# Cosine attention into a token and channel MLP on one core: PSUM split anew, and a pair's scores in one group

## The chip, the core and the metric

The kernel runs on one core of a Trainium2 chip. A core has a matrix engine (TensorE, "PE" in the profile), two engines that read its results from PSUM (VectorE, "DVE", and ScalarE, "ACT"), a fourth engine that works in SBUF alone (GpSimd, "POOL"), and SyncE ("SP"), whose queue issues most of the DMAs. Each engine works through its own list of instructions in order; semaphores hold an instruction back until what it needs is there. PSUM has eight banks of 128 partitions by 512 fp32 numbers. The metric is device time in microseconds (us).

## The reference, cut to what matters

```python
def _attn_ref(q, k, v, tau):              # 8 batches, 12 heads, 448 tokens, 64 columns
    q_n = q / (np.linalg.norm(q, axis=-1, keepdims=True) + 1e-06)
    k_n = k / (np.linalg.norm(k, axis=-1, keepdims=True) + 1e-06)
    scores = np.matmul(q_n, k_n.transpose(0, 1, 3, 2)) / tau
    ...
    attn = np.exp(scores)
    attn = attn / (np.sum(attn, axis=-1, keepdims=True) + 1e-09)
    return np.matmul(attn, v)

def _moe_ref(x, w_tok1, w_tok2, w_ch1, w_ch2):   # x: 8 x 448 x 768, all heads side by side
    xt = x.transpose(0, 2, 1)
    h = np.maximum(xt @ w_tok1, 0.0) @ w_tok2    # token MLP, 448 -> 256 -> 448
    u = x + h.transpose(0, 2, 1)
    h2 = np.maximum(u @ w_ch1, 0.0) @ w_ch2      # channel MLP, 768 -> 1536 -> 768
    return u + h2
```

## The kernel before

The attention part works on 48 pairs of heads, six to a batch. The 448 tokens are three blocks of 128 and a rest of 64; the two heads' rests stand together as one block of 128 partitions. For one pair p the stages are:

- **Norms.** Squares of q and k (L176; on ScalarE or GpSimd), their sums on VectorE (`sums`, L189), four small ScalarE activations that turn a sum into one over the norm (`rnorms`, L197 to L200), and the scaling to fp16 on GpSimd (`scaled`, L207).
- **Transposes** of the scaled q and k: on TensorE through a PSUM tile `pst` and a VectorE copy (`next_qk`) for pairs below 15, by DMA afterwards (`dma_tpose`).
- **Scores** (`score`, L297): for each block c of three, two matmuls, one for each head, into the two banks of a tile `psS`. A head has 64 columns, so each of these matmuls uses 64 of the 128 rows of the array, and the two of a block stand side by side in it. One exp on ScalarE empties both banks (L298). The rests go through a full-height matmul into `psX` (L304) and an exp of their own (L305).
- **Values** (`pv`, L318 and L320): 28 matmuls, in two halves of 14, each into a tile `psO` of one bank; a column of ones beside v gives the sums of the exps. VectorE takes the reciprocal (L323) and multiplies (L324), which gives x of the pair.
- **Token MLP**: `m_tok1` (tile `psR`, L338, a VectorE max) and `m_tok2` (tile `psU`, L357, then a VectorE copy or add into `ut`).

Once all six pairs of a batch have their `ut`, the channel MLP of the batch is put into a queue of units: 12 of `m_ch1` (six matmuls of 448 columns into `psG`, L385, a Relu on ScalarE, L387) and 6 to 9 of `m_ch2` (twelve matmuls of up to 384 columns into `psF`, L400, an add on VectorE, L403). `feed` takes units out of that queue and puts them between the steps of later pairs, until a budget of matmul time is used up.

The order on every engine is the order in which the program is written (the schedule is a manual one). Loop i = 0 to 49 takes one pair's scores at a time: the scores of pair i, the values of pair i-1, the first token matmul of pair i-2, the second of the same pair or of pair i-3. Three stretches are written differently: i below 6, where no channel MLP is to be had yet; i = 6 (`FIRST`); and from there on. Before the change, blocks 0 and 1 of the scores stand at the head of a pair, and block 2 later, after the values and some channel work; from i = 12 (`JOIN`) on, block 2 of an even pair stands beside block 0 of the next.

PSUM is shared out as follows. Pool `ps` has four tiles of one bank for everything but scores: `pst`, `psX`, `psO`, `psR`, `psU`, `psG`, `psF`, in turn. Pool `ps2` has two tiles of two banks for `psS`. A tile is handed out again in order: the first matmul of the fifth tile of `ps` waits until the first one's reader is done.

Of the kernel before, what the change touches and what calls it, by code (L numbers as in the profile page):

```python
# [7 lines left out]
FP32 = mybir.dt.float32  # L8
FP16 = mybir.dt.float16
# [13 lines left out]
def kernel(  # L23
# [12 lines left out]
    nc = tc.nc  # L36
# [30 lines left out]
    att = ctx.enter_context(tc.tile_pool(name="att", bufs=3))  # L67
    mix = ctx.enter_context(tc.tile_pool(name="mix", bufs=2))
    outp = ctx.enter_context(tc.tile_pool(name="outp", bufs=2))
    ps = ctx.enter_context(tc.tile_pool(name="ps", bufs=4, space=bass.MemoryType.PSUM))  # L70
    ps2 = ctx.enter_context(tc.tile_pool(name="ps2", bufs=2, space=bass.MemoryType.PSUM))

    id16 = cst.tile([P, P], FP16, name="id16")
    tiny = cst.tile([P, 1], FP32, name="tiny")
# [225 lines left out]

    def score_x(p):
        qk, pt = qks[p], pts[p % 2]
        psX = ps.tile([P, 512], FP32, name=f"psX_{p}", tag="b")
        nc.tensor.matmul(psX[:, 0:S], qk[:, P * NC:P * (NC + 1)], qk[:, 512:512 + S], start=True, stop=True)  # L304
        nc.scalar.activation(out=pt[:, PX:PX + S], in_=psX[:, 0:S], func=AF.Exp, scale=inv_tau)  # L305

    def pv(p, a):
        n, j = p // HP, p % HP
        vt, vx, pt = vts[n % NV], vxs[n % NV], pts[p % 2]
        if a == 0:  # L310
            xs[p] = att.tile([P, NC + 1, P], FP16, name=f"x_{p}", tag="x")
        psO = ps.tile([P, 2, 2 * E1], FP32, name=f"psO_{p}_{a}", tag="b")
        for mm in range(2):
            lo = P * (2 * a + mm)
            for g in range(2):
                for c in range(NC):
                    at = (2 * c + g) * S + lo
                    nc.tensor.matmul(psO[:, mm, E1 * g:E1 * (g + 1)], pt[:, at:at + P], vt[:, 2 * j + g, c, 0:E1],  # L318
                                     start=(g == 0 and c == 0), stop=False)
            nc.tensor.matmul(psO[:, mm, :], pt[:, PX + lo:PX + lo + P], vx[:, j, 0:2 * E1], start=False, stop=True)  # L320
        rec = att.tile([P, 2, 2], FP32, name=f"rec_{p}_{a}", tag="rec")
        o = psO[:].rearrange("p m (g e) -> p m g e", g=2)
        nc.vector.reciprocal(out=rec[:], in_=o[:, :, :, E])  # L323
        nc.vector.tensor_tensor(out=xs[p][:, 2 * a:2 * a + 2, :].rearrange("p m (g e) -> p m g e", g=2),  # L324
                                in0=o[:, :, :, 0:E], in1=_bcast_free(rec[:], E), op=ALU.mult)


# [4 lines left out]
                                    in_=xs[p][:].rearrange("p c d -> p (c d)"))  # L332

    def m_tok1(p):
        psR = ps.tile([P, TT, P], FP32, name=f"psR_{p}", tag="b")
        for tt in range(TT):
            for m in range(NC + 1):
                nc.tensor.matmul(psR[:, tt, :], w1t[:, m, tt * P:(tt + 1) * P], xs[p][:, m, :],  # L338
                                 start=(m == 0), stop=(m == NC))
        rs[p] = att.tile([P, TT, P], FP16, name=f"r_{p}", tag="r")  # L340
        nc.vector.tensor_scalar_max(out=rs[p][:], in0=psR[:], scalar1=0.0)

    def m_tok2(p):
        b, dt = p // NPAIR, p % NPAIR
        odd = b % 2
        if b // 2 not in pairt:
            pairt[b // 2] = (mix.tile([P, DT, 2 * S], FP16, name=f"ut16_{b // 2}", tag="ut16"),
                             mix.tile([P, CT, 2 * S], FP16, name=f"gt16_{b // 2}", tag="gt16", bufs=1))  # L350
        ut = pairt[b // 2][0][:, dt, S * odd:S * (odd + 1)]
        psU = ps.tile([P, S], FP32, name=f"psU_{p}", tag="b")
        by_dma = p in X_DMA
        lo = 0 if odd else XR
        cols = [XR * odd + P * c for c in range(NC)] + [0 if odd else SM]
        for tt in range(TT):
            nc.tensor.matmul(psU[:], rs[p][:, tt, :], w2t[:, tt, lo:lo + S], start=(tt == 0),  # L357
                             stop=by_dma and tt == TT - 1)
        if not by_dma:
            for c in range(NC + 1):  # L360
                w = P if c < NC else XR
                nc.tensor.matmul(psU[:, cols[c]:cols[c] + w], xs[p][:, c, :], id16[:, 0:w],
                                 start=False, stop=(c == NC))
            nc.vector.tensor_copy(out=ut, in_=psU[:])
        else:
            for u0, x0, w in ((0, SM, XR), (XR, 0, SM)) if odd else ((0, 0, S),):
                nc.vector.tensor_tensor(out=ut[:, u0:u0 + w], in0=psU[:, u0:u0 + w], in1=xTs[p][:, x0:x0 + w],  # L367
                                        op=ALU.add)
# [79 lines left out]


    FIRST = NPAIR  # L450

    JOIN = 2 * NPAIR
    early_sq = {3: 0, 4: 1, 5: 1, 6: 3, 7: 4, 8: 5, 9: 5, 10: 6, 11: 7, 12: 8, 13: 9, 14: 9, 15: 10, 16: 11, 17: 11}
    sq_slot = {p: early_sq.get(p, p - 6) for p in range(3, NP_ALL)}
    sq_at = at(sq_slot)
# [15 lines left out]
    cast_at = at({n: {1: 2, 2: 6}.get(n, 3 * n - 2) for n in range(1, NHALF)})  # L471
    tok_slot = {p: FIRST if p in (FIRST - 2, FIRST - 1) else p + 2 for p in range(NP_ALL)}
    tok_at = at(tok_slot)
    tok2_slot = {p: max(tok_slot[p] + (p in X_DMA), 3) for p in range(NP_ALL)}
    tok2_at = at(tok2_slot)

    ut_at = at({p: 8 + p // 3 if p < NPAIR else 12 + (p - NPAIR) // 2 if p < 2 * NPAIR else t + 1
# [31 lines left out]
    with tc.manual_schedule():  # L509
# [77 lines left out]
        for i in range(NP_ALL + 2):  # L587
# [17 lines left out]
            def next_qk(p):  # L605
                if p < min(DMA_FROM, NP_ALL):
                    qk_copy(p, tpose(p))
# [13 lines left out]

            if i == FIRST:
                next_sq([9])
                m_tok1(i - 2)
                pv(i - 1, 0)
                pv(i - 1, 1)
                tok2(i - 2)
                m_tok1(i - 1)
                next_qk(i)
                tok2(i - 1)  # L630
                norm_sums(8)
                feed(0.0, 1000.0)
                score(i, 0)
                rnorms(2, 21, 45)
                score(i, 1)
                norm_sums(9)
                feed(0.0, 1000.0)
            elif 0 < i < NP_ALL and not (i > JOIN and i % 2):
                score(i, 0, 2 if i < 4 else 0)
                score(i, 1)  # L640
            for p in sum_at.get(i, ()):
                norm_sums(p)
            if i != FIRST:
                norm_rn()

            if i >= FIRST:
                for p in sc_at.get(i, ()):
                    norm_scale(p, nc.gpsimd)
            if i < FIRST or i >= 2 * NPAIR:
                next_sq([p for p in sq_at.get(i, ()) if p != 9])  # L650
            if i < FIRST:
                for p in sc_at.get(i, ()):
                    norm_scale(p, nc.gpsimd)
            for n in cast_at.get(i, ()):
                cast_v(n)
            if i in (2, 5):
                weights_ch1(i // 4)
            if i in (7, 8):
                weights_ch2(i - 7)

            if i < FIRST:
                if i:
                    pv(i - 1, 0)
                if i:
                    score(i, 2)
                    score_x(i)
                if i + 1 < FIRST:
                    next_qk(i + 1)
                for p in tok_at.get(i, ()):
                    m_tok1(p)  # L670
                if i:
                    pv(i - 1, 1)
                for p in tok2_at.get(i, ()):
                    tok2(p)
            elif i == FIRST:
                score(i, 2)
                score_x(i)
                feed(0.0, 1000.0)
                rnorms(3, 0, 21)
                next_qk(i + 1)  # L680
                next_sq(sq_at[i])
                norm_sums(10)
                feed(0.0, 1000.0)
            else:
                feed(quota * 0.25)
                next_qk(i + 1)
                if i <= NP_ALL:
                    pv(i - 1, 0)
                for p in tok_at.get(i, ()):
                    m_tok1(p)  # L690
                feed(quota * 0.25, 400.0)
                ahead = i >= JOIN and i % 2 == 0
                if ahead and i <= NP_ALL:
                    pv(i - 1, 1)
                if i < NP_ALL:
                    if i > JOIN and i % 2:
                        score(i, 1)
                    score(i, 2)
                    if ahead:
                        score(i + 1, 0)  # L700
                    score_x(i)
                if i < 2 * NPAIR:
                    next_sq(sq_at[i])
                for p in tok2_at.get(i, ()):
                    tok2(p)
                feed(quota * 0.25)
                if i <= NP_ALL and not ahead:
                    pv(i - 1, 1)
                if i < 2 * NPAIR:
                    for p in sq_at[i]:  # L710
                        norm_sums(p)
                feed(quota * 0.25)
            if i == 2:
                place_w2()
        for p in ut_at.get(NP_ALL + 2, ()):
# [37 lines left out]
```

## Time and profile before

| | |
|---|---|
| Median of 12 runs | 399.3 us (398.94 to 401.0) |
| The profiled execution | 401.0 us, of which the span from first to last instruction is 399.1 us |
| TensorE busy | 386.3 us, 3658 matmuls |
| ScalarE, VectorE, GpSimd busy | 225.9, 205.0, 208.5 us |
| Mean granted TensorE clock | 0.987 |

The profile's page lists busy time by engine, the span in 40 slices of 10 us (each digit is a tenth, 9 is 90% or more), and the costliest groups of instructions as "line engine op out<-in shapes xcount | busy us, mean ns of one | idle time before them". A timeline row gives start, length and engine of a group of like instructions. Matmuls overlap: the next starts before the last is through, so the length of one (353 ns for 448 columns) is not what it costs; the distance between starts is. Where this text says "step", it is that distance.

### The profile page before, as it was taken

The page shows a single profiled execution, that of the slowest core. Times are in us where ns is not written, and L with a number is a line of the kernel's source. Part 1 is how long each engine was busy: PE and PEld are TensorE (multiplying, and loading weights), DVE is VectorE, ACT ScalarE, POOL GpSimd, SP SyncE. Part 2 cuts the span into 40 slices and gives each one's busy share as a digit, 9 for nine tenths or more (in the row PEclk, how much of TensorE's full clock was granted, in tenths as well). Part 3 has the DMA queues.
Part 4 walks back from the last instruction along what each step waited for, and adds up shares of the span by engine and source line. Part 5 has one row for each costly group of instructions (what it writes and reads, how often), then busy time and mean ns, then how long its engine had stood idle before and what let it go on. Part 6 is the DMA issues. An engine that isn't in the chain of part 4 may idle for free.

```text
span 399.1 us, 9143 instructions
## 1 busy us (share of the span) xinstructions
PE 386.3 (97%) x3658; PEld 228.3 (57%) x3658; DVE 205.0 (51%) x464; ACT 225.9 (57%) x407; POOL 208.5 (52%) x306
## 2 busy tenths in 40 slices
PE   7599999999999999999999999999999999999997
PEld 2256556566556565565565565565555565566554
DVE  5678778665453655446444645546544443243022
ACT  5888599753676447655657436665657435520410
POOL 4967495968292949576682919567682500000000
PEclk9779999999999999999999999999999999999999
DMA  8999999999797599898997599889953553013013
GB/s 219 254 232 245 239 228 208 208 240 270 159 182 159 137 252 196 182 201 185 230 204 178 96 263 208 166 192 195 212 109 72 137 105 68 15 41 110 10 39 118
DMA packets 137482, 67.51 MB, mean 169 GB/s; under 512 B 93216, under 2 KB 133984, under 8 KB 137440
## 3 DMA queue, kind: packets, MB, share of 16 engines
q1 hardware_dynamic: 133264, 61.36, 70.4%
q0 software_dynamic: 3632, 5.18, 7.5%
q8 instruction: 28, 0.46, 0.5%
q10 hardware_dynamic: 544, 0.39, 0.3%
q14 instruction: 14, 0.11, 0.1%
HBM read 43.38 MB, written 11.01 MB: 136 GB/s over the span
## 4 chain that ended last, share of the span: by engine, by line
PE 44%; POOL 24%; issue 17%; DMA 6%; ACT 5%; DVE 2%; SPq 1%; ACTq 0%; POOLq 0%; DVEq 0%
PE psF L400 16%; PE psG L385 13%; POOL kq L207 9%; POOL sq L176 8%; PE psO L318 4%; PE psS L297 3%; DMA xv<-in_v_dram 3%; POOL sqx L176 2%; ACT pt L298 2%; PE psR L338 2%; POOL kq L218 2%; DMA xq<-in_q_dram 2%; PE psU L357 2%; POOL vt L164 2%; PE psX L304 1%
## 5 line engine op out<-in xcount | busy, mean ns | idle before, releaser
L298 ACT ACTIVATE pt<-psS 128x896 f16<-128x896 f32 x141 | 122.1, 916 | 65.3 <-PE psS L297 65.2
L385 PE MATMUL psG<-ut,wc1t 128*128 128x448 f16 x576 | 120.7, 353 | 0.0
L400 PE MATMUL psF<-wc2t,gt 128*128 128x384 f16 (+2 forms) x684 | 116.3, 323 | 0.0
L387 ACT ACTIVATE gt<-psG 128x448 f16<-128x448 f32 x96 | 52.5, 547 | 74.5 <-PE psG L385 74.3
L207 POOL TENSOR_TENSOR kq<-km,rn 128x384 f16<-128x384 f32 x47 | 39.6, 842 | 99.7 <-ACT rn L200 98.4
L400 PEld LDWEIGHTS <-gt 128*128 128x128 f16 x684 | 64.8, 98 | 40.5 <-issue 1.1
L385 PEld LDWEIGHTS <-wc1t 128*128 128x128 f16 x576 | 53.2, 98 | 46.5 <-issue 4.4
L403 DVE TENSOR_TENSOR ost<-psF,ur 128x384 f32<-128x384 f32 (+2 forms) x57 | 31.3, 549 | 78.1 <-PE psF L400 78.1
L318 PEld LDWEIGHTS <-pt 128*128 128x128 f16 x1152 | 53.5, 98 | 15.6 <-issue 3.9
L318 PE MATMUL psO<-vt,pt 128*128 128x65 f16 x1152 | 58.4, 195 | 0.0
L189 DVE TENSOR_REDUCE ssq<-sq 128x12 f32<-128x768 f32 (+1 forms) x49 | 45.2, 931 | 17.9 <-POOL sq L176 12.8
L297 PE MATMUL psS<-qk 64*128 64x448 f16 x282 | 41.6, 363 | 2.6 <-ACT pt L298 2.5
L324 DVE TENSOR_TENSOR x<-psO,rec 128x256 f16<-128x256 f32 x96 | 40.7, 424 | 3.3
L320 PE MATMUL psO<-vx,pt 128*128 128x130 f16 x192 | 42.3, 220 | 0.0
L323 DVE RECIPROCAL rec<-psO 128x4 f32<-128x4 f32 x96 | 17.1, 178 | 48.0 <-PE psO L320 47.8
L207 POOL TENSOR_TENSOR kq<-qm,rn 128x384 f16<-128x384 f32 x47 | 38.9, 828 | 0.0
L176 POOL TENSOR_TENSOR sq<-km 128x384 f32<-128x384 f32 x42 | 34.4, 822 | 2.7 <-DMA km<-in_k_dram 2.5
L338 PE MATMUL psR<-x,w1t 128*128 128x128 f16 x384 | 29.4, 219 | 0.1
L367 DVE TENSOR_TENSOR ut<-psU,xT 128x448 f16<-128x448 f32 (+2 forms) x39 | 17.6, 477 | 20.1 <-PE psU L357 20.0
L357 PE MATMUL psU<-w2t,r 128*128 128x448 f16 x96 | 25.9, 353 | 0.7 <-DVE x L324 0.4
L305 ACT ACTIVATE pt<-psX 128x448 f16<-128x448 f32 x48 | 26.5, 553 | 0.0
L176 POOL TENSOR_TENSOR sq<-qm 128x384 f32<-128x384 f32 x30 | 24.7, 823 | 0.8
(75 smaller groups left out, 322.9 us busy)
## 6 DMA issues: line engine op xcount, KB each, us to landing
vm<-in_v_dram SPq DMA_DIRECT2D x16, 576.0 KB, 5.3
out_dram<-ost SPq DMA_DIRECT2D x23, 384.0 KB, 3.9
qm<-in_q_dram SPq DMA_DIRECT2D x15, 576.0 KB, 6.1
km<-in_k_dram SPq DMA_DIRECT2D x15, 576.0 KB, 5.1
wc1t<-in_moe_w_ch_dram POOLq DMA_DIRECT2D x2, 1152.0 KB, 13.7
wc2t<-in_moe_w_ch_dram POOLq DMA_DIRECT2D x2, 1152.0 KB, 15.0
out_dram<-ost SPq DMA_DIRECT2D x9, 192.0 KB, 3.2
xq<-in_q_dram SPq DMA_DIRECT2D x7, 192.0 KB, 5.3
```

The costliest lines, as they stand in the source:

```text
L176: eng.tensor_tensor(out=out, in0=src, in1=src, op=ALU.mult)
L189: nc.vector.tensor_reduce(out=ssqs[p // HP % 3][:, lo + 6 * a0:lo + 6 * a1], in_=sq[p][:, a0:a1].rearrange("p a g e -> p (a g) e"), axis=A ...
L207: eng.tensor_tensor(out=kqs[n % 2][:, j, a, 0:NC, :].rearrange("p c (g e) -> p g c e", g=2), in0=src, in1=_bcast_free(rn, E), op=ALU.mult)
L297: nc.tensor.matmul(psS[:, g, 0:S], qk[r, P * c:P * (c + 1)], qk[r, 512:512 + S], start=True, stop=True)
L298: nc.scalar.activation(out=pt[:, 2 * S * c:2 * S * (c + 1)].rearrange("p (g s) -> p g s", g=2), in_=psS[:, :, 0:S], func=AF.Exp, scale=inv ...
L318: nc.tensor.matmul(psO[:, mm, E1 * g:E1 * (g + 1)], pt[:, at:at + P], vt[:, 2 * j + g, c, 0:E1], start=(g == 0 and c == 0), stop=False)
L320: nc.tensor.matmul(psO[:, mm, :], pt[:, PX + lo:PX + lo + P], vx[:, j, 0:2 * E1], start=False, stop=True)
L324: nc.vector.tensor_tensor(out=xs[p][:, 2 * a:2 * a + 2, :].rearrange("p m (g e) -> p m g e", g=2), in0=o[:, :, :, 0:E], in1=_bcast_free(re ...
L338: nc.tensor.matmul(psR[:, tt, :], w1t[:, m, tt * P:(tt + 1) * P], xs[p][:, m, :], start=(m == 0), stop=(m == NC))
L385: nc.tensor.matmul(psG[:], wc1t[:, dt, ct * P:(ct + 1) * P], ut[:, dt, sp], start=(dt == 0), stop=(dt == DT - 1))
L387: nc.scalar.activation(out=gt[:, ct, sp], in_=psG[:], func=AF.Relu)
L400: nc.tensor.matmul(psF[:, 0:w], gt[:, ct, lo:lo + P], wc2t[:, ct, P * i0:P * i1], start=(ct == 0), stop=(ct == CT - 1))
```

## The change

The two pools are cut differently: `ps` keeps two tiles of one bank, for `psG`, `psF`, `pst` and, in the first two batches, `psU`; `ps2` has three tiles of two banks, in turn for `psS`, `psX`, `psO`, `psR` and the later `psU`. The three blocks of a pair's scores stand in one group, and `JOIN` is gone. `pv` is no longer in halves: all 28 matmuls go into one two-bank tile, with one reciprocal and one multiplication. The rest of a pair's order is written anew around that: the exp of `psX`, the norms (`norm_rn`, `norm_scale`), the squares and the casts of v change places, `psU` of the first pairs moves one pair later, and the portions of `feed` are cut differently. The matmuls themselves are the same 3658.

```diff
-    ps = ctx.enter_context(tc.tile_pool(name="ps", bufs=4, space=bass.MemoryType.PSUM))
-    ps2 = ctx.enter_context(tc.tile_pool(name="ps2", bufs=2, space=bass.MemoryType.PSUM))
+    ps = ctx.enter_context(tc.tile_pool(name="ps", bufs=2, space=bass.MemoryType.PSUM))
+    ps2 = ctx.enter_context(tc.tile_pool(name="ps2", bufs=3, space=bass.MemoryType.PSUM))
...
     def score_x(p):
-        psX = ps.tile([P, 512], FP32, name=f"psX_{p}", tag="b")
+        psX = ps2.tile([P, 2, 512], FP32, name=f"psX_{p}", tag="s")[:, 0, :]
...
-    def pv(p, a):
+    def pv(p):
...
-        psO = ps.tile([P, 2, 2 * E1], FP32, name=f"psO_{p}_{a}", tag="b")
-        for mm in range(2):
+        psO = ps2.tile([P, NC + 1, 256], FP32, name=f"psO_{p}", tag="s")
+        for m in range(NC + 1):
...
     def m_tok1(p):
-        psR = ps.tile([P, TT, P], FP32, name=f"psR_{p}", tag="b")
+        psR = ps2.tile([P, 2, 512], FP32, name=f"psR_{p}", tag="s")[:, 0, 0:TT * P].rearrange("p (t d) -> p t d", t=TT)
...
-        psU = ps.tile([P, S], FP32, name=f"psU_{p}", tag="b")
+        psU = (ps.tile([P, 512], FP32, name=f"psU_{p}", tag="b") if b < 2 else
+               ps2.tile([P, 2, 512], FP32, name=f"psU_{p}", tag="s")[:, 0, :])[:, 0:S]
...
-    tok2_slot = {p: max(tok_slot[p] + (p in X_DMA), 3) for p in range(NP_ALL)}
+    tok2_slot = {p: min(p + 3, FIRST) if p < NPAIR else tok_slot[p] + (p in X_DMA) for p in range(NP_ALL)}
...
             if i == FIRST:
                 next_sq([9])
+                rnorms(2, 21, 33)
+                norm_scale(7, nc.gpsimd)
+                pv(i - 1)
                 m_tok1(i - 2)
-                pv(i - 1, 0)
-                pv(i - 1, 1)
+                tok2(i - 3)
+                next_qk(i)
                 tok2(i - 2)
                 m_tok1(i - 1)
-                next_qk(i)
+                score(i, 0)
+                score(i, 1)
+                score(i, 2)
                 tok2(i - 1)
...
-            elif 0 < i < NP_ALL and not (i > JOIN and i % 2):
+            elif 0 < i < NP_ALL:
                 score(i, 0, 2 if i < 4 else 0)
                 score(i, 1)
+                score(i, 2)
...
             if i < FIRST:
+                for p in tok2_at.get(i, ()):
+                    tok2(p)
+                if i == 3:
+                    next_qk(i + 1)
                 if i:
-                    pv(i - 1, 0)
+                    pv(i - 1)
                 if i:
-                    score(i, 2)
                     score_x(i)
-                if i + 1 < FIRST:
+                if i in (0, 1, 2, 4):
                     next_qk(i + 1)
                 for p in tok_at.get(i, ()):
                     m_tok1(p)
-                if i:
-                    pv(i - 1, 1)
-                for p in tok2_at.get(i, ()):
-                    tok2(p)
...
             else:
-                feed(quota * 0.25)
+                if i >= 2 * NPAIR:
+                    next_sq(sq_at.get(i, ()))
+                if i < DMA_FROM:
+                    norm_next()
+                    casts()
+                fed[0] = 0.0
+                feed(quota * 0.3, 900.0 if i < DMA_FROM else 1800.0)
+                if i < NP_ALL:
+                    score_x(i)
+                if i >= DMA_FROM:
+                    norm_next()
+                    casts()
                 next_qk(i + 1)
                 if i <= NP_ALL:
-                    pv(i - 1, 0)
+                    pv(i - 1)
+                both = [p for p in tok2_at.get(i, ()) if p in tok_at.get(i, ())]
+                if not both:
+                    feed(quota * 0.3)
                 for p in tok_at.get(i, ()):
                     m_tok1(p)
-                feed(quota * 0.25, 400.0)
-                ahead = i >= JOIN and i % 2 == 0
-                if ahead and i <= NP_ALL:
-                    pv(i - 1, 1)
-                if i < NP_ALL:
-                    if i > JOIN and i % 2:
-                        score(i, 1)
-                    score(i, 2)
-                    if ahead:
-                        score(i + 1, 0)
-                    score_x(i)
                 if i < 2 * NPAIR:
                     next_sq(sq_at[i])
+                if both:
+                    feed(quota * 0.3, 900.0)
                 for p in tok2_at.get(i, ()):
                     tok2(p)
-                feed(quota * 0.25)
-                if i <= NP_ALL and not ahead:
-                    pv(i - 1, 1)
                 if i < 2 * NPAIR:
                     for p in sq_at[i]:
                         norm_sums(p)
-                feed(quota * 0.25)
+                feed(quota * 0.4, 900.0 if i >= 2 * NPAIR else 0.0)
```

`norm_next` is `norm_rn` and then the pair's `norm_scale`; `casts` holds the casts of v and the loads of the channel weights, which stood in the loop before.

## The prediction

> **What bounds the kernel now.** First the busy times and the clock on the page, then the groups of work:
>
> ```profile
> PE 386.3 (97%) x3658; PEld 228.3 (57%) x3658; DVE 205.0 (51%) x464; ACT 225.9 (57%) x407; POOL 208.5 (52%) x306
> ...
> PEclk9779999999999999999999999999999999999999
> ...
> L298 ACT ACTIVATE pt<-psS 128x896 f16<-128x896 f32 x141 | 122.1, 916 | 65.3 <-PE psS L297 65.2
> L324 DVE TENSOR_TENSOR x<-psO,rec 128x256 f16<-128x256 f32 x96 | 40.7, 424 | 3.3
> L323 DVE RECIPROCAL rec<-psO 128x4 f32<-128x4 f32 x96 | 17.1, 178 | 48.0 <-PE psO L320 47.8
> ```
>
> TensorE is busy 97% and the other engines about half, but overlapping matmuls hide what a step costs. So next the timeline of TensorE, in the steady part:
>
> ```profile
> 200.52 0.22 PE L320 MATMUL psO<-vx,pt 128*128 128x130 f16 x1
> 200.57 0.61 PE L338 MATMUL psR<-x,w1t 128*128 128x128 f16 x8
> ...
> 202.59 0.22 PE L320 MATMUL psO<-vx,pt 128*128 128x130 f16 x1
> 202.74 0.55 PE L297 MATMUL psS<-qk 64*128 64x448 f16 x4
> 203.23 0.36 PE L304 MATMUL psX<-qk 128*128 128x448 f16 x1
> 203.43 0.54 PE L357 MATMUL psU<-w2t,r 128*128 128x448 f16 x2
> 203.80 3.57 PE L385 MATMUL psG<-ut,wc1t 128*128 128x448 f16 x18
> 207.21 0.35 PE L318 MATMUL psO<-vt,pt 128*128 128x65 f16 x6
> ```
>
> Read the starts. 18 `psG` take 3.41 us, 189 ns each; `psX` to `psU` is 0.20. That is 448 columns at full rate, with no wait between tiles: TensorE is the bound and runs gapless. From 80 us to the end the starts of single matmuls show five gaps of over 0.1 us, 1.8 us in all. One thing costs extra without being a wait: going in and out of the half-height scores. `psO` to `psR` takes 0.055 us, the same `psO` to `psS` 0.150. Single starts give 285 against 189 out of `psG`, 258 against 162 out of `psF`, and 281 against 189 from the last score to whatever follows. So a run of scores costs 95 on entry and 93 on leaving, **188 ns a run**, whatever stands before it.
>
> The early pairs differ; some one-microsecond stretches, and two rows of ScalarE's timeline:
>
> ```profile
> 18.00:19.00 1.00, 0.00 (x0) 0.50 1.15 187
> ...
> 24.00:25.00 1.00, 1.00 (x14) 0.50 0.98 216
> 25.00:26.00 1.00, 1.00 (x12) 0.99 0.74 165
> ```
> ```profile
> 27.82 1.73 ACT L298 ACTIVATE pt<-psS 128x896 f16<-128x896 f32 x2 [0.38 <-PE psS L297]
> 29.43 0.52 ACT L174 ACTIVATE sq<-qm 128x384 f32<-128x384 f32 x1
> ```
>
> (Third and later columns of the first: TensorE busy, granted clock, DMA share, GB/s.) The clock is 0.50 from 14.9 to 25.0 us; TensorE had idled. Two exps in a row take 1.73 us: a step of 0.815, then 0.916 to the end; squares and norms stand in the same queue.
>
> **The change, part by part.**
>
> *Scores in one group.* Counting by the two instruction orders: 78 runs of half-height matmuls before (two a pair for pairs 1 to 11, 1.5 a pair for 12 to 47, two in pair 0), 49 after. 29 x 0.188 = **-5.45 us**, all on the bound engine. [...] The trace measured the step itself, so I take 0.188.
>
> *One tile for a pair's values.* VectorE does 48 reciprocals of 128x8 (about 185 ns) and 48 products of 128x512 in place of 96 and 96. From 256 to 512 columns I add 1.05 ns a column (L367: 623 at 448, 547 at 384, so 1.2; L403 384 against 256: 556 - 424, so 1.03): 690 ns. Saved 48 x (1204 - 875) = 15.8 us of VectorE, worth 0: it is half idle. The price is lateness: x of the pair is ready 0.9 us after the last `psO`, not 0.6. Readers of x come a pair later, so only the ring waits for it.
>
> *The ring of three.* A tile now waits for the reader three tiles back. Steady order: S0 S1 S2 X O R U, so X waits for exp S0, O for exp S1, R for exp S2, U for exp X, the next S0 for O's product, S1 for R's max, S2 for U's add. The hardest steady pair (14 of them put two `psG` ahead of X), from S0 = 0: scores end 0.76, G 1.9, G 3.03, X 3.23, O 4.23 (24 x 0.033 + 4 x 0.056), R 4.68, then U. ScalarE: exps 0.41 to 2.95, two Relus (547 each, step 0.43) to 3.8, exp X to 4.3. U finds its tile free at 4.3, needs it at 4.68: 0.4 to spare. VectorE: O seen 4.4, product done 5.3, max 5.7, add 6.4; the next S2 comes at 7.8. With `psF` ahead of X there is more room. **0**; if that cover goes, ScalarE at 916 and 547 without overlap puts exp X at 4.85: 0.17 x 14 = +2.4.
>
> *Two banks for the channel MLP.* Unit k waits for the reader of k-2, at least one unit later (1.13 us against a Relu of 0.55): 0 in steady state, 0.2 once at pair 12, where a `psF` meets `psU` in the same pool.
>
> *Pairs 1 to 5.* No channel work stands between S2 and the values. O waits for exp S0, X for S1, R for S2, and the next S1 for exp X, which now stands behind three exps and the norms and squares. Pair 4: exps to 2.95, four norm activations 1.0, a square 0.5, exp X to 4.95; pair 5's S1 wants its tile at 3.9: 1.1 late. Pair 1: O waits for exp S0 (19.1, as late as S2 waits now), but then 28 matmuls come, not 14: 0.4 late. Pair 3: 0.1. Walked so, the values of pair 5 start at 40.75 (now 40.72) with a `psU` (0.57) and a `psR` (0.45) still undone; the 5 runs saved (0.94) are spent too: **+2.0**. Bounds: 0 (waits as now) to +3.5.
>
> *Pairs 6 to 11.* Relus queue behind exps and norms with two `psG` banks. Pair 6's eight norm activations hold back a Relu and the exps of 7: X of 7 waits 0.75, its next `psG` 0.3; pairs 8 and 10 (norms 1.1 before the Relu) 0.6 and 0.4; 0.15 in pair 6: +2.2. Today's gaps there are 2.0; 0.75 (q and k of pair 12 come late from GpSimd) stay, the rest goes, since the transposes and scores that wait there move: -1.25. **+0.95**; bounds -0.5 to +2.5.
>
> *Pairs 12 to 47.* Half of today's 1.8 us of gaps should go with three score tiles, less the 0.2: **-0.7**.
>
> *Moved steps.* From pair 12 GpSimd takes squares before scaling, and from 15 the norms come after exp X, about 2 us later in a pair. Scaling of a half's first pair ends about 9 us after its norm pair began (norms done 5.4, five GpSimd rows 3.5); SyncE's transpose of it, issued at 6.8, then blocks SyncE some 2 us: behind it wait x and u transposes, loads issued three pairs ahead, and stores. q and k are needed two pairs (13 us) on. The last scaling of the three ends 3 us before its transpose. Casts of v are needed three pairs on. The four weight loads stay in their pairs. All 0; if GpSimd fell 5 us behind, the next norms would stand in ScalarE ahead of the Relus, some 0.5 us for each of 11 halves.
>
> Sum: -5.45 + 2.0 + 0.95 - 0.7 = -3.2. The profiled execution took 401.0 (span 399.1), so 397.8 for it; set against the median 399.3, which lies 1.7 lower, **396.1**.
>
> **Rivals.** (1) *ScalarE paces the ring.* For it: seven tiles in three places, four of them behind exps. Against: 0.4 us to spare. With the 2.4 above: 398.5. (2) *The clock stays low*, and the kernel is slower. [...] (3) *The switch isn't what costs 188 ns*, but the first matmul after a semaphore, and each new order pays it elsewhere. Against: `psO` to `psR` enters a new tile too, at 0.055. Then 399.3 + 2.0 + 0.95 - 0.7 = 401.5. (4) *The early pairs don't wait* (VectorE and ScalarE catch up): 396.1 - 2.5 = 393.6.
>
> **Numbers.** Forecast 0.52, rival 1 0.18, rival 2 0.20, rival 3 0.04, rival 4 0.06. A measurement tells 0.2% (0.8 us) from no change. Faster: 0.52 + 0.06 + two thirds of rival 1 = 0.70; same: the rest of rival 1 and 0.03 of rival 2 (two windows); slower 0.17 + 0.04 = 0.21. The likeliest case alone spans 394.0 to 398.2 (early bounds). The range, 393.5 to 400.5, leaves out the worse part of rivals 2 and 3, about 0.18.
>
> **What would show it.** Right: 49 runs of scores with 0.15 before and 0.28 after each; no gap of over 0.1 us between matmuls from 100 us on but a few; idle before `psO` of pairs 1 to 4 put down to the exp, and before S1 of pair 5; clock 1.0 from 25 to 28 us. Wrong: regular gaps before `psU` or S0 in the steady part, a clock of 0.50 beyond 28 us, or SyncE's waits on the scaling growing past 10 us.

## The result, and the profile after

The changed kernel takes **395.0 us** (median of 8 runs, 394.37 to 395.82) against 399.3 before (32 runs on the same chip): ratio 0.9888, 95% interval 0.9872 to 0.9903, so 1.1% or 4.3 us faster. The forecast was 396.1. The profiled execution took 394.9 us, its span 393.1, mean clock 0.991.

The page of the changed kernel, busy times, clock and groups:

```profile
PE 379.1 (96%) x3658; PEld 229.2 (58%) x3658; DVE 193.5 (49%) x368; ACT 225.9 (57%) x411; POOL 209.3 (53%) x306
...
PEclk9699999999999999999999999999999999999999
...
L298 ACT ACTIVATE pt<-psS 128x896 f16<-128x896 f32 x141 | 119.0, 921 | 66.1 <-PE psS L297 65.9
...
L322 DVE RECIPROCAL rec<-psO 128x8 f32<-128x8 f32 x48 | 9.9, 207 | 80.8 <-PE psO L318 80.7
...
L323 DVE TENSOR_TENSOR x<-psO,rec 128x512 f16<-128x512 f32 x48 | 33.2, 691 | 1.7
```

TensorE issues the same 3658 matmuls and is 7.2 us less busy. VectorE has 96 instructions fewer and 11.5 us less work: the wide product takes 691 ns (worked out: 690), the reciprocal 207 (185).

The timeline of TensorE in the steady part, one pair:

```profile
201.57 1.30 PE L385 MATMUL psG<-ut,wc1t 128*128 128x448 f16 x6
202.80 0.74 PE L297 MATMUL psS<-qk 64*128 64x448 f16 x6
203.48 2.44 PE L385 MATMUL psG<-ut,wc1t 128*128 128x448 f16 x12
205.76 0.35 PE L304 MATMUL psX<-qk 128*128 128x448 f16 x1
205.95 0.35 PE L316 MATMUL psO<-vt,pt 128*128 128x65 f16 x6
...
208.07 0.61 PE L337 MATMUL psR<-x,w1t 128*128 128x128 f16 x8
208.51 0.54 PE L357 MATMUL psU<-w2t,r 128*128 128x448 f16 x2
```

One run of six scores where there were two runs of four and two. `psG` to `psS` is 1.23 us: 5 x 0.189 inside the tile and 0.285 on entry. Entry and exit cost what they did (the step out of the last score is 0.281 again), but come once. `psX` to `psO` is 0.19, `psR` to `psU` 0.44: no wait. From 101.4 us to the end no single step is more than 0.06 us above full rate (0.189 us for 448 columns, 0.162 for 384, 0.056 for 128).

What TensorE waited for, costliest first (us in total, times, longest), without the first two lines, which belong to the start-up:

```profile
PE psU L357 <- DVE w2t L150: 1.3, 1, 1.3
PE psF L400 <- DVE ost L403: 1.3, 1, 1.3
PE psO L316 <- ACT pt L298: 0.9, 2, 0.6
...
PE psS L297 <- ACT pt L305: 0.5, 2, 0.4
```

The last two are of the waits foreseen in the early pairs. The first two were not foreseen. The first is `psU` of pair 0 at 27.9 us, which waits for VectorE's placing of the second token weight. The second is seen in the timeline of all engines at pairs 12 and 13:

```profile
87.44 2.53 SPq L376 DMA_TRANSPOSE ur<-ut  x2
...
90.06 1.90 SPq L410 DMA_DIRECT2D out_dram<-ost  x2
...
93.40 0.61 PE L337 MATMUL psR<-x,w1t 128*128 128x128 f16 x8
...
94.68 0.56 DVE L403 TENSOR_TENSOR ost<-psF,ur 128x384 f32<-128x384 f32 x1 [3.54 <-DMA out_dram<-ost]
...
95.30 2.11 PE L400 MATMUL psF<-wc2t,gt 128*128 128x384 f16 x12 [1.29 <-DVE ost L403]
```

Read it upwards. `psF` needs one of the two banks of the channel MLP; the bank's reader, VectorE's add into `ost`, waits 3.54 us because both `ost` buffers are still being stored; the store was issued at 90.06, behind two `ur` transposes in SyncE's queue. VectorE meanwhile holds back everything else. It costs 1.45 us of TensorE.

**Where the time went.** For every step from one matmul to the next I took what it lasted above full rate, with 188 ns for each run of scores counted as normal, and summed by stretch. The comparison is with a profiled execution of the unchanged kernel whose half-clock stretch is as long as after's (399.43 us, span 397.6, clock 0.991); the one shown before the prediction had three microseconds more of it.

| | before | after | difference | predicted |
|---|---|---|---|---|
| 29 score runs x 0.188 | | | -5.45 | -5.45 |
| 0 to 40 us (pairs 0 to 5) | 11.7 | 13.8 | +2.1 | +2.0 |
| 40 to 80 us (pairs 6 to 11) | 2.8 | 1.7 | -1.1 | +0.95 |
| 80 us to the end | 2.1 | 2.3 | +0.2 | -0.7 |
| sum | | | -4.25 | -3.2 |

The spans differ by 4.5; a quarter of a microsecond is not placed. So the mechanism is the one foreseen and two of the stretches are not.

### The profile page after: what moved, and what is told of

Read it like the earlier page. It is cut to its first block, busy times and chain, and to the rows that moved or that the text cites. A ratio compares the mean times of both kernels' runs of the same rounds, so it can differ in the third digit from the quotient of the medians.

```text
span 393.1 us, 9085 instructions
## 1 busy us (share of the span) xinstructions
PE 379.1 (96%) x3658; PEld 229.2 (58%) x3658; DVE 193.5 (49%) x368; ACT 225.9 (57%) x411; POOL 209.3 (53%) x306
## 4 chain that ended last, share of the span: by engine, by line
PE 86%; ACT 5%; DVE 4%; DMA 2%; SPq 1%; issue 1%; DVEq 0%
PE psF L400 28%; PE psG L385 27%; PE psO L316 9%; PE psS L297 7%; PE psR L337 5%; PE psU L357 4%; PE psO L318 3%; ACT pt L298 2%; PE psX L304 2%; DMA out_dram<-ost 1%; DMA km<-in_k_dram 1%; PE psU L362 1%; PE pst L239 1%; DVE ost L403 1%; DVE ssq L189 1%
## 5 line engine op out<-in xcount | busy, mean ns | idle before, releaser
L298 ACT ACTIVATE pt<-psS 128x896 f16<-128x896 f32 x141 | 119.0, 921 | 66.1 <-PE psS L297 65.9
L385 PE MATMUL psG<-ut,wc1t 128*128 128x448 f16 x576 | 119.5, 353 | 0.2
L387 ACT ACTIVATE gt<-psG 128x448 f16<-128x448 f32 x96 | 51.1, 557 | 73.4 <-PE psG L385 73.4
L316 PEld LDWEIGHTS <-pt 128*128 128x128 f16 x1152 | 50.8, 98 | 8.6 <-issue 2.5
L316 PE MATMUL psO<-vt,pt 128*128 128x65 f16 x1152 | 53.1, 194 | 1.2 <-ACT pt L298 0.9
L322 DVE RECIPROCAL rec<-psO 128x8 f32<-128x8 f32 x48 | 9.9, 207 | 80.8 <-PE psO L318 80.7
L297 PE MATMUL psS<-qk 64*128 64x448 f16 x282 | 35.9, 357 | 1.3 <-DVE qk L257 0.7
L323 DVE TENSOR_TENSOR x<-psO,rec 128x512 f16<-128x512 f32 x48 | 33.2, 691 | 1.7
L337 PEld LDWEIGHTS <-w1t 128*128 128x128 f16 x384 | 23.8, 97 | 2.0 <-issue 0.3
```

Of the source, the lines that this page charges most:

```text
L297: nc.tensor.matmul(psS[:, g, 0:S], qk[r, P * c:P * (c + 1)], qk[r, 512:512 + S], start=True, stop=True)
L298: nc.scalar.activation(out=pt[:, 2 * S * c:2 * S * (c + 1)].rearrange("p (g s) -> p g s", g=2), in_=psS[:, :, 0:S], func=AF.Exp, scale=inv ...
L316: nc.tensor.matmul(psO[:, m, E1 * g:E1 * (g + 1)], pt[:, at:at + P], vt[:, 2 * j + g, c, 0:E1], start=(g == 0 and c == 0), stop=False)
L385: nc.tensor.matmul(psG[:], wc1t[:, dt, ct * P:(ct + 1) * P], ut[:, dt, sp], start=(dt == 0), stop=(dt == DT - 1))
L387: nc.scalar.activation(out=gt[:, ct, sp], in_=psG[:], func=AF.Relu)
```

## The experiments

### The price of a switch: one full-height matmul put into the scores

From pair 7 on, 41 pairs, one full-height 128-column matmul, whose result the scores overwrite: ahead of the run (nothing is split), or inside it.

```
 def score(p, c, fill=0, one=False):
...
+        if one:
+            busy(psS[:, 0, 0:P], 1)
...
             elif 0 < i < NP_ALL:
-                score(i, 0, 2 if i < 4 else 0)
+                score(i, 0, 2 if i < 4 else 0, one=i > FIRST)
                 score(i, 1)
                 score(i, 2)
```

and in the second kernel, with the same helper:

```
                 score(i, 0, 2 if i < 4 else 0)
                 score(i, 1)
-                score(i, 2)
+                score(i, 2, one=i > FIRST)
```

> The changed kernel with one more full-height matmul of 128 columns, ahead of block 0 of the scores, for pairs 7 to 47 (41 of them); it writes into the tile of block 0, which the scores then overwrite. It stands where the array is at full height anyway. Control for the next kernel: 41 x 0.056 = +2.3 us, 397.3, by every theory.

> The changed kernel with the same extra matmul of 128 columns between blocks 1 and 2 of the scores. If going in and out of half height costs 188 ns a run, each pair now has two runs: 41 x (0.056 + 0.188) = +10.0 us, 405.0, which is 7.7 us over the control. If the 188 ns belong to something else (the first matmul after a wait, a new tile), it stands where the control does, 397.3.

Measured: ahead 396.61 us (5 runs, 396.13 to 397.63), inside 406.11 (4 runs, 405.34 to 407.19). TensorE's timeline, ahead:

```profile
201.80 1.30 PE L387 MATMUL psG<-ut,wc1t 128*128 128x448 f16 x6
202.93 0.22 PE L232 MATMUL psS<-id 128*128 128x128 f16 x1
203.08 0.74 PE L299 MATMUL psS<-qk 64*128 64x448 f16 x6
203.76 2.44 PE L387 MATMUL psG<-ut,wc1t 128*128 128x448 f16 x12
```

and inside:

```profile
200.06 2.43 PE L387 MATMUL psG<-ut,wc1t 128*128 128x448 f16 x12
202.42 0.55 PE L299 MATMUL psS<-qk 64*128 64x448 f16 x4
202.91 0.23 PE L232 MATMUL psS<-id 128*128 128x128 f16 x1
203.07 0.36 PE L299 MATMUL psS<-qk 64*128 64x448 f16 x2
203.36 2.44 PE L387 MATMUL psG<-ut,wc1t 128*128 128x448 f16 x12
```

From the start of the last `psG` matmul before the scores (5 and 11 steps of 0.189 after the row's start) to the first one after them: 1.015 us ahead, 1.226 inside by single starts, with the same instructions. The split costs 0.211, a little more than 0.188. Over 41 pairs that is 8.7 of the 9.5 us between the two kernels; the profile of the second also has one stall of 1.56 us near 65 us. The kernel with the matmul ahead is 1.6 us slower than the changed kernel, not 2.3 as expected; in its profile the stall of `psF` is 0.8 us shorter (0.68 against 1.45). In the splitting nothing waits for a semaphore that did not before, and the same tiles are used: rival 3, that the first matmul after a wait is what costs, falls. What the array does in this time, no run shows.

### The old split of PSUM under the new order

```
-    ps = ctx.enter_context(tc.tile_pool(name="ps", bufs=2, space=bass.MemoryType.PSUM))
-    ps2 = ctx.enter_context(tc.tile_pool(name="ps2", bufs=3, space=bass.MemoryType.PSUM))
+    ps = ctx.enter_context(tc.tile_pool(name="ps", bufs=4, space=bass.MemoryType.PSUM))
+    ps2 = ctx.enter_context(tc.tile_pool(name="ps2", bufs=2, space=bass.MemoryType.PSUM))
...
-        psX = ps2.tile([P, 2, 512], FP32, name=f"psX_{p}", tag="s")[:, 0, :]
+        psX = ps.tile([P, 512], FP32, name=f"psX_{p}", tag="b")
...
+        for a in range(2):
+            psO = ps.tile([P, 2, 256], FP32, name=f"psO_{p}_{a}", tag="b")
...
```

`psR` and `psU` are taken from `ps` in the same way; the order of the work is that of the changed kernel.

> The changed kernel's order of work with the PSUM split of before: four one-bank tiles for everything but scores (the values in two tiles of 14 matmuls again), two two-bank tiles for scores. Theory: the split is what lets three blocks of scores stand together; with two tiles block 2 waits for the exp of block 0, which is seen 1.4 us after S0 starts, 1.0 us after block 2 could have gone. For the 41 pairs from 7 on that is +41 us, less what the early pairs and the four banks give back: about 435. Rival: the order alone made the gain, the split is worth nothing: 395.

Measured: 439.93 us (4 runs), ratio 1.1014 (1.0977 to 1.1052). What TensorE waits for:

```profile
PE psS L297 <- ACT pt L298: 43.1, 47, 1.9
```

and one pair of its timeline:

```profile
201.50 0.55 PE L297 MATMUL psS<-qk 64*128 64x448 f16 x4
202.87 0.36 PE L297 MATMUL psS<-qk 64*128 64x448 f16 x2 [0.82 <-ACT pt L298]
```

With two score tiles the third block waits for the exp of the first, once in each of 47 pairs. The grouping is worth 5.45 us and needs the third tile; without it the same order is 45 us slower than the changed kernel. So the grouping can't be had without the new split. The new split under the old order was not run.

### One tile for a pair's values, evacuated in halves

```
-        nc.vector.reciprocal(out=rec[:], in_=o[:, :, :, E])
-        nc.vector.tensor_tensor(out=xs[p][:].rearrange("p m (g e) -> p m g e", g=2),
-                                in0=o[:, :, :, 0:E], in1=_bcast_free(rec[:], E), op=ALU.mult)
+        for h in (slice(0, 2), slice(2, 4)):
+            nc.vector.reciprocal(out=rec[:, h, :], in_=o[:, h, :, E])
+            nc.vector.tensor_tensor(out=xs[p][:, h, :].rearrange("p m (g e) -> p m g e", g=2),
+                                    in0=o[:, h, :, 0:E], in1=_bcast_free(rec[:, h, :], E), op=ALU.mult)
```

> The changed kernel with the values' reciprocal and product in two halves again, of the same two-bank tile: 48 x 0.33 = 15.8 us more of VectorE. Theory: VectorE's work there is hidden, 395.0 within 0.8. Rival: VectorE's saving is what made the changed kernel better than was forecast: 396 or more.

Measured: 399.72 us (10 runs, 398.09 to 402.36), ratio 0.9993 (0.996 to 1.0026). A miss, and the largest of the study: emptying the one tile in halves costs 4.7 us by the medians, 4.2 by the two ratios, about as much as the whole change gains. It is not the form of before, though: there the first half had a tile of its own and was emptied before the second was through; here both halves wait for the last matmul. What the merge is worth against that form, no run shows. All engines, around the dearest place:

```profile
61.75 0.88 POOL L158 DMA_DIRECT2D wc2t<-in_moe_w_ch_dram  x1
...
62.14 3.14 DVE L176 TENSOR_TENSOR sqx<-xk 128x192 f32<-128x192 f32 x1
...
62.66 0.84 POOL L207 TENSOR_TENSOR kq<-km,rn 128x384 f16<-128x384 f32 x1
63.45 0.83 POOL L207 TENSOR_TENSOR kq<-qm,rn 128x384 f16<-128x384 f32 x1
...
64.24 0.82 POOL L176 TENSOR_TENSOR sq<-km 128x384 f32<-128x384 f32 x1
65.21 0.61 DVE L365 CAST ut<-psU 128x448 f16<-128x448 f32 x1
...
65.87 0.49 PE L239 MATMUL pst<-id,kq 128*128 128x128 f16 x6 [1.73 <-DVE ut L365]
```

In pair 8 VectorE reaches the square of the k rests of pairs 12 to 14 late, beside three operations of GpSimd; it takes 3.14 us (0.98 in the changed kernel, as low as 0.35 before it), the evacuation of `psU` behind it is late, and TensorE stands 1.73 us (1.9 against full rate). After that idle time TensorE's clock is 0.50 from 67.1 to 70.6 us: eight `psR` steps take 0.107 us where 0.056 is full rate, then five `psG` steps 0.374 where it is 0.189; with the end of the values 1.6 us more. Besides: 0.7 in pairs 4 and 5, and eight waits of 0.2 before a `psU`, 1.6, since the tile is free 0.24 later (1.18 us from the first reciprocal to the last product in pair 8, against 0.94); the stall of `psF`, on the other hand, is 0.9 shorter here. Together 4.9 of the 5.2 us by which its span is longer than that of the changed kernel. Its five runs with a mean clock of 0.991 and above have the median 398.8; the five at 0.987 and 0.983 took 399.7 to 402.4, so about 0.9 of the 4.7 comes with more time at half clock.

So "half idle" was the wrong view of VectorE. In windows of ten microseconds (columns: window, length, busy us of TensorE, its weight load, VectorE, ScalarE, GpSimd with their instructions, clock, DMA share, GB/s) the changed kernel shows

```profile
20.00:30.00 10.00, 7.69 (x109) 5.17 (x108) 9.00 (x15) 9.05 (x18) 8.04 (x12) 1.00 1.15 256
30.00:40.00 10.00, 8.88 (x145) 6.40 (x143) 7.88 (x15) 8.94 (x18) 7.47 (x11) 1.00 1.13 256
```

VectorE is 79 to 90% busy there (from 60 to 80 us 83%), though 49% over the span. The square ends 0.2 us after the third GpSimd row, and the 0.98 us one of the changed kernel (60.43 to 61.41) 0.2 us after a GpSimd row that ends at 61.21. But the square starts half a microsecond before the first of the three; GpSimd is issuing a weight load then (61.75 to 62.63). Whether GpSimd's operations or its load hold the square up, no run shows, and none separates that from VectorE's own lateness.

### The clock: the unchanged kernel repeated, and a warm start

Rival 2 is that the clock stays low. In the traces it stands at 0.50 for 10.2 us (the execution profiled before the prediction, mean clock 0.987), 6.8 us (the changed kernel, and the unchanged one run again, both 0.991) and 3.4 us (the kernel with the matmul ahead of the scores, 0.996): three, two and one times 3.4 us, called windows below. The unchanged kernel was run ten times, to read its times against its clocks; and in the changed kernel TensorE was kept busy in pair 0 by 13 matmuls of 512 columns that nothing reads:

```
         score_main0(2)
+        busy(w, 9)
         tpose_x(0, pst)
...
+        busy(w, 4)
         score_rest0()
```

> The kernel before, unchanged, for its clock in several executions. Theory: the execution profiled before the prediction (401.0 us, mean granted clock 0.987) was one whose half-clock stretch lasted one window longer than usual; most executions stand at 399.2 with a mean clock near 0.991, and the times go with the clock, about 1.7 us for 0.004. Rival: the clock is the same in all, and the 1.7 us between 401.0 and the median have another cause.

> The changed kernel with 13 more 512-column matmuls that nobody reads, nine behind block 2 of pair 0 and four before its rests, where TensorE stands idle today, so that it doesn't idle before 14 us and the clock stays at 1.0. [...] By the executions of the kernel before, where 1.000, 0.995 and 0.991 stand at 399.0, 399.2 and 399.4 us: -0.4, 394.6, since ScalarE and the loads pace that stretch.

Measured: unchanged 399.23 us. At a mean clock of 1.000 it took 398.99; at 0.995 and 0.996, one window, 399.08 to 399.73; at 0.991, two, 399.15, 399.43, 399.47 and once 401.07. Two windows are worth some 0.4 us; at the expected 1.7 for each it would be 3.4. A third goes with more: the unchanged kernel's four runs at 0.987 beside the other experiments took 400.3 to 402.3, the one profiled before the prediction 401.0. But four of those at 0.991 took 400.4 to 402.9 too, so a long run isn't always a matter of the clock, and that the third window is the cause is not shown. The expectation of 1.7 us for each 0.004 can hold for that last window at most. Warm: 395.12 (4 runs), at the clocks 0.996, 1.000, 0.996, 1.000 for 395.49, 393.76, 396.68, 394.75. Against the changed kernel's 395.0 that is no change; even the two runs at full clock lie 0.7 below it on average. Windows of the changed kernel (columns: window, length, TensorE's busy us and matmuls, clock, DMA share, GB/s):

```profile
13.00:14.00 1.00, 0.23 (x6) 0.50 1.25 250
...
19.00:20.00 1.00, 1.00 (x18) 0.61 1.19 241
...
27.00:28.00 1.00, 0.07 (x1) 1.00 1.04 181
```

and of the warm one:

```profile
19.00:20.00 1.00, 1.00 (x15) 0.50 1.19 278
...
27.00:28.00 1.00, 0.13 (x2) 1.00 1.12 250
```

The half clock moved from 12.9 to 19.8 us to 18.8 to 22.2 and became one window shorter, and nothing came of it: the idle microsecond at 27 us, where TensorE waits for VectorE, is there in both. The window at 67 us of the kernel with halves cost 1.6 us. An estimate from its steps, which take twice as long there (0.374 us against 0.189), is half of 3.4 us, 1.7. The first two windows here are hardly paid.

### The stall at 27 us: `psU` of pair 0 later

In the changed kernel `psU` of pair 0 stands ahead of the values of pair 2 and waits 1.4 us for the weight. Here it is moved to the end of pair 3:

```
-                for p in tok2_at.get(i, ()):
-                    tok2(p)
                 if i == 3:
                     next_qk(i + 1)
+                else:
+                    for p in tok2_at.get(i, ()):
+                        tok2(p)
...
                 for p in tok_at.get(i, ()):
                     m_tok1(p)
+                if i == 3:
+                    tok2(0)
```

> The changed kernel with psU of pair 0 put back to the end of pair 3, where the kernel before has it. In the changed kernel's trace TensorE stands 1.33 us before it at 26.6 us, for VectorE's placing of w_tok2. Theory: the stall goes, and as ScalarE paces pairs 1 to 5 about a third comes back behind other waits: -1.0, 394.0. Rival: those pairs are paced by ScalarE and the loads alone, and the stall was hidden: 395.0.

Measured: 394.91 us (4 runs, ratio 0.9886, 0.9855 to 0.9918), no change that four runs can tell: the rival, not the theory. The stall is gone from the list of waits; in its place a `pst` is 0.63 us late at 27.9 us, and the values of the first pairs wait 1.4 us for exps where it was 0.9. So TensorE is not the bound there: what it doesn't wait for at one tile it waits for at the next.

### The stall at 94 us: a third output buffer

```
-    outp = ctx.enter_context(tc.tile_pool(name="outp", bufs=2))
+    outp = ctx.enter_context(tc.tile_pool(name="outp", bufs=3))
```

> The changed kernel with three output tiles in place of two (pool outp). In the changed kernel's trace VectorE waits 3.5 us at pair 13 for an earlier store before it may empty a psF, and TensorE stands 1.45 us. Theory: that stall goes, 1.3 to 1.45 us less, 393.6. Rival: the wait is passed on to the next tile, or the store's delay shows elsewhere: 395.0.

Measured: 394.22 us (4 runs), ratio 0.9847 (0.9806 to 0.9889). The same place:

```profile
92.60 0.56 DVE L403 TENSOR_TENSOR ost<-psF,ur 128x384 f32<-128x384 f32 x1 [0.65 <-PE psF L400]
...
94.20 0.61 PE L337 MATMUL psR<-x,w1t 128*128 128x128 f16 x8
...
94.65 2.11 PE L400 MATMUL psF<-wc2t,gt 128*128 128x384 f16 x12
```

The add no longer waits for the store and `psF` starts 0.45 after `psR`, at once. The cause of the stall is shown; the gain of 0.8 us in the medians lies within the intervals of the two ratios.

### The changed kernel again, the transposes at full height, and both mends

If a half-height matmul pays the switch, so do the last transposes of a pair's q and k where TensorE does them, 15 times, 64 rows high. Made full height, they write 64 columns more that nothing reads:

```
-        nc.tensor.transpose(pst[:, P * 7:P * 7 + XR], kq[0:XR, p % HP, 1, NC], id16[0:XR, 0:XR])
+        nc.tensor.transpose(pst[:, P * 7:P * 8], kq[:, p % HP, 1, NC], id16[:])
```

> The changed kernel itself, beside the next two on the same chip: 395.0, and 98.9% of the kernel before.

> The changed kernel with the transposes of the 64 rest rows of q (15 of them, the only other half-height matmuls) taken at full height: the 64 further rows are zeros that are there already, and nobody reads the 64 further columns. Theory of the switch: in and out again cost 0.095 + 0.10 us each, the longer matmul 0.028 more, so 15 x 0.17 = 2.5 us, of which the six in pairs 0 to 5 are partly behind ScalarE's waits: -1.5 to -2.5 against the changed kernel, 393.0. If the 188 ns were not the change of height: 395.0 or a little more.

> Both edits: the transposes at full height and three output tiles. If the stall for the store (1.45 us at pair 13) and the switches lie on the same bound and don't hide each other, the gains add: 393.0 - 1.0 = 392.0, better than both kernels. If the store's stall is a matter of that execution, 393.0.

Measured on one chip: changed kernel 394.91 us (ratio 0.9878, 0.9862 to 0.9893), full-height transposes 394.17 (0.9863, 0.9844 to 0.9882), these with the third output buffer **392.76** (5 runs, 391.72 to 394.34; 0.9828, 0.9805 to 0.9851). TensorE's timeline in the changed kernel, then with full-height transposes, each followed by the values:

```profile
57.30 0.22 PE L243 MATMUL pst<-id,kq 128*128 128x128 f16 x1
57.45 0.20 PE L244 MATMUL pst<-id,kq 64*128 64x64 f16 x1
57.59 0.36 PE L316 MATMUL psO<-vt,pt 128*128 128x65 f16 x6
```

```profile
58.59 0.22 PE L243 MATMUL pst<-id,kq 128*128 128x128 f16 x1
58.65 0.22 PE L244 MATMUL pst<-id,kq 128*128 128x128 f16 x1
58.70 0.35 PE L316 MATMUL psO<-vt,pt 128*128 128x65 f16 x6
```

By single starts, steps of 0.056 and 0.056 where the changed kernel has 0.151 and 0.132: 0.17 saved 15 times, 2.6 us. Only 0.7 arrives in the medians, less than expected and within the two intervals. Ten of these transposes lie in the first 60 us, and there the trace shows about 2 us more of lost time, as with `psU` above; the five behind them are worth 0.85. Both mends together are 2.15 us faster than the changed kernel, with intervals that don't overlap, and 6.9 than the first; 392.0 was expected if the gains add.

## Why the prediction came out right, and where not

**Scores in one group, -5.45: right,** in size and cause. The entry and exit steps after are those before, and splitting one run again costs 0.211 a pair.

**Pairs 1 to 5, +2.0: right in sum (+2.1), not in its places.** The waits for exps in the first pairs came, at most 0.6 each, but S1 of pair 5 waited 0.5 where 1.1 was worked out, and the walk left out `psU` of pair 0, which waits 1.4 for the weight's placing. Moving that stall gained nothing that four runs can tell. With the places wrong, that the sum came out is in part luck, and in part that other engines pace the whole stretch. Rival 4, that the early pairs don't wait, falls.

**Pairs 6 to 11, +0.95: wrong by 2 us** (-1.1). The step that failed is "pairs 8 and 10 ... 0.6 and 0.4" and "its next `psG` 0.3". X of pair 7 waited 0.67 (0.75 predicted) and one step of pair 6 lost 0.18 (0.15); the others did not come. (Two more steps of pair 6, at a `psU`, lose 0.41 and 0.31, which the walk did not have; as much of the small losses of before is gone.) I had the two banks of the channel MLP taken strictly in turn, as the part on the kernel says. All engines of the changed kernel in pair 8:

```profile
55.63 1.31 PE L385 MATMUL psG<-ut,wc1t 128*128 128x448 f16 x6
...
56.97 0.50 PE L239 MATMUL pst<-id,kq 128*128 128x128 f16 x6
...
59.00 0.53 ACT L387 ACTIVATE gt<-psG 128x448 f16<-128x448 f32 x1
59.03 1.30 PE L385 MATMUL psG<-ut,wc1t 128*128 128x448 f16 x6
```

The Relu of the tile of 55.63 is late, as worked out: it begins at 59.00 behind exps. The next `psG` starts at 59.03, while that Relu reads. In turn, it would have had the Relu's bank, since the transposes' tile took the other; so it must have the transposes' bank, whose reader is done at 58.35. Of the three waits that did not come, the `psG` of pairs 7 and 10 do the same: they start at 53.73 and 70.78 us, while Relus run from 53.36 to 53.93 and from 70.68 to 71.21. These are the only three of the 170 tiles of that pool behind 40 us that start so. A late reader blocked only the tile that was given its bank. Besides, that the 0.75 us "stay" failed: the gap of before for q and k of pair 12 went too; why, no run shows.

**Pairs 12 to 47, -0.7: wrong by 0.9, with errors in both directions.** The late gaps all went (2.1 us from 130 us on, in six gaps and not five; half was predicted): three score tiles seem to cover more than was credited. Against that three small waits of 0.24, 0.24 and 0.31 between 86 and 101 us, where one of 0.2 was foreseen, and the stall of 1.45 at 94 us. That one breaks **"Moved steps", "All 0"**, which named SyncE's queue and the stores behind it and then only asked when q and k are needed, not when the output buffer is. (SyncE's longest wait on the scaling is 8.3 us, under the 10 that were named as a sign.)

**The ring of three, 0: right.** No gap before `psU` or S0 in the steady part, so rival 1 did not happen.

**One tile for the values, VectorE's saving "worth 0": wrong** in its reason. The walk of the ring used the merged durations (product done at 5.3, max at 5.7), so the forecast did not suffer; but with the tile emptied in halves the kernel is 4.7 us slower. The reason given, that VectorE is half idle, is a mean over stages.

**Rival 2** was given a fifth of the chance and carried most of the slower side. The clock was 0.50 from 12.9 to 19.8 us (6.8 us; 15.4 to 22.2 in the unchanged kernel it is compared with), and the idle microsecond at 27 us didn't lower it again. No run shows the price at which its windows enter the chances: in the unchanged kernel the first two cost 0.2 us each, in the kernel with halves the one at 67 us cost 1.6. **Rival 3** falls with the full-height matmul.

So the forecast was 1.1 us too high: 2.05 too much for pairs 6 to 11, 0.9 too little for the pairs behind them. That the two cancel in part is luck.

## What to carry to other kernels

Count the changes between full-height and half-height matmuls on a TensorE that bounds, transposes of a partial block included, and price them by single starts: group them only as far as there are PSUM tiles to hold the group (here 0.188 us for each run of scores saved, and 45 us lost without the third tile). Price a saved instruction on a helper engine by its busy share in the stage where its results are waited for (VectorE's 79 to 90% here), not over the span (49%); and when a store moves back in a queue, ask when its buffer is wanted again. A stall on an engine that another one paces reappeared here in good part when it was removed: three repairs in the first 60 us brought between nothing and a third of what the trace seemed to offer.

## What was not expected of the hardware

- In these traces a switch between full-height and half-height matmuls costs 0.093 to 0.096 us each way; where a single full-height matmul splits a run, 0.211 for both. The 64-row transposes pay it as well: steps of 0.151 and 0.132 against 0.056 at full height.
- In the unchanged kernel the first two windows at half clock, 3.4 us each, cost 0.2 us each; a third goes with 1.4 more by the medians (0.987 against 0.991), though its share in that is not shown; one window at 67 us of the kernel with halves cost 1.6, where its steps were twice as long.
- A square of 128x192 on VectorE, 0.35 us at its shortest (kernel before), took 3.14 beside three GpSimd operations in a row, and ended 0.2 us after the third.
